# Gated values in three buffers, y's differences one by one, and the third output unit loaded into the first one's place

## The chip, the cores and the metric

The kernel runs on one core of a Trainium2 chip. Its time is the device time in microseconds, the median of several runs. A profile is one more execution, recorded by the hardware profiler; its times hold for that execution.

The engines: TensorE (PE: matrix products, PEld: the weight loads that run beside them), VectorE (DVE), ScalarE (ACT), GpSimd (POOL) and SyncE (SP), whose queue issues nearly all transfers here. Each engine takes its instructions in the order written and waits at the first that is not ready. The order is the program's own (`manual_schedule`), and nothing rearranges it.

## The reference

Three stages on 4608 tokens of 512 values. The inputs are float32.

```
a   = softmax(q k^T / 8) v              # chunks of 64 tokens, 8 heads of 64
x   = reshape(a)                        # 4608 x 512
h   = x @ w_in                          # 4608 x 1024
s   = h * softmax(h)
y   = ((s - mean) / sqrt(var + 1e-6) * g_ln) @ w_out      # 4608 x 512
u   = silu(y @ w_gate) * (y @ w_val)                      # 4608 x 1536
out = u @ w_out2                                          # 4608 x 512
```

Every product is split for precision: each factor is kept as a high part and the rest, and three of the four products of the parts are added up (`PASSES`). The two products of the last stage are in addition formed by Strassen's scheme in Winograd's form: seven block products in place of eight, from sums and differences of blocks.

## The kernel before, in words

Up to about 315 us the kernel forms attention, h and the normalized s; to 523 us it multiplies by w_out (`y_run`, in runs of 24 products of 128x128 by 128x384) and meanwhile prepares the weights of the last stage. The change concerns what comes then.

**The gated stage, 72 steps (`step`, L925).** The tokens lie in six groups s of 768 and the 1536 columns in twelve blocks f; a step (s, f) makes one block of u for one group. TensorE does seven products of six matmuls each, into the banks psA, psC, psB, psD, psA, psC, psD. The fifth, sixth and seventh add to what the first, second and fourth left in the same bank, so the fifth waits until ScalarE has copied psA to p1 (L934) and the seventh until VectorE has read psD (L941). p1 is one buffer: L934 waits until the step before has read it for the last time (L953). The rest of a step runs beside the products: VectorE adds (L939, L941), GpSimd adds (L942), ScalarE takes the sigmoid of psA into the first half of a tile u (L944), VectorE multiplies (L945), adds psC into the buffer that L942 has read (L948), a second sigmoid (L949), and VectorE ends with L951 to L954. The tile u then goes to memory by one transfer that SyncE issues in the next step (`u_store`, L923). u has two buffers, so L944 waits until the store of two steps ago has read its tile.

**The factors.** The weights of blocks 0, 1 and 2 are loaded once and kept (wc, `cache_load`); the others stream through a ring of three tiles (ws, `w_load`), one load issued whenever a step has used its tile. Group 0 takes blocks 3 to 11 and then 0, 1, 2; the groups after it take 0 to 11. In group 5 all twelve stream, since the space of wc is then used for the factors of the output.

**Beside the steps.** While group s runs, y of group s+1 is loaded (`y_load`) and made into the seven operands of the scheme (`y_units`): for each half kk four differences on GpSimd, called as one unit of four instructions (`sums`, L822), then seven units `split(i, x)`, each with a copy on ScalarE (L825) and a subtraction on VectorE (L826). Sixteen units are spread over the steps, one to three in a step, called after its own instructions:

```
k = -(-len(todo) // ((FT if s < NSG - 2 else 7) - n)) if todo else 0
for x in todo[:k]:
    x()
```

y of group 0 is prepared in the same way during the last eight `y_run`s, two units to a run. The third weight is converted in 24 pieces, one in two steps, from step 0 on: `v_load`, `v_mag` (ScalarE, then L95 on GpSimd), `v_bits` (L101 and L109 on VectorE, then L130 on GpSimd), `v_store`.

**The output stage, 54 units (`unit`).** Unit n = (g, p) reads u of 512 tokens and two blocks from memory (`x_load`), forms four sums on VectorE (`x_sums`, L1042), the high parts on ScalarE (`x_high`, L1048) and the rest on VectorE (`x_low`, L1053), and multiplies (L1119). The x of a unit lies in one of four places: `halves[0]` and `halves[1]` in the tile ry, which y's preparation used before, and two in `hold`, a part of the tile work, which takes the space of the last group's y operands and is free only when the last step's products are done. Unit n takes place n mod 4. Units 0 and 1 are prepared during the last four steps, units 2 and 3 after them. `x_low(n)` ends by calling `x_load(n + 4)`. The loop at the end prepares ahead of the products:

```
for n in range(NU):
    x_high(n + 2)
    x_sums(n + 3)
    x_low(n + 2)
    for i in range(2):
        unit(n, i)
```

Of the kernel before, what the change touches and what calls it, by code (L numbers as in the profile page):

```python
# [8 lines left out]
F32 = mybir.dt.float32  # L9
# [14 lines left out]
def attn_moe_moe2_kernel(  # L24
# [136 lines left out]
    def y_run(wB, i0, i1, ps, sb, ptags=("y",), stag="ysb", queue=nc.scalar):  # L161

        for i in range(i0, i1):
            u, n = divmod(i, NY)
            m, d = divmod(u, KD)
            f, (a, b) = n // 3, PASSES[n % 3]
            if n == 0:
                ys[u] = ps.tile([P, TOK], F32, tag=ptags[u % len(ptags)], name="y")
            nc.tensor.matmul(  # L169
                ys[u], lhsT=wB[:, f, a, d * P:(d + 1) * P], rhs=lnT[m][:, b, f, :],  # L170
                start=(n == 0), stop=(n == NY - 1),
            )
            if n == NY - 1:
                ysb = sb.tile([P, TOK], F32, tag=stag, name="ysb", bufs=3 if stag == "osb" else 2)
                nc.scalar.activation(out=ysb, in_=ys.pop(u), func=AF.Copy)  # L175
                queue.dma_start(out=y_dram[m][d], in_=ysb)
# [588 lines left out]
    with ExitStack() as ph2:  # L765
# [6 lines left out]
        )  # L772
        ry = cpa.tile([P, 3, 4, TOK], F32, tag="ry", name="ry")
        rawy, tt = ry[:, 0:2], ry[:, 2]
        yk = {0: cpa.tile([P, NS, 2, 2, TOK], F32R, tag="yka", name="yka")}
# [35 lines left out]
        def y_units(s, kks=(0, 1)):  # L811

            if s not in yk:
                yk[s] = yk_tile(s)
            dst, units = yk[s], []
            for kk in kks:
                b11, b12, b21, b22 = (rawy[:, kk, i] for i in range(4))
                t1, t2, t3, t4 = (tt[:, i] for i in range(4))

                def sums(b11=b11, b12=b12, b21=b21, b22=b22):  # L820
                    for o, p, q in ((t1, b12, b11), (t2, b22, t1), (t3, b22, b12), (t4, b21, t2)):
                        nc.gpsimd.tensor_tensor(out=o, in0=p, in1=q, op=ALU.subtract)  # L822

                def split(i, x, kk=kk):
                    nc.scalar.activation(out=dst[:, i, 0, kk], in_=x, func=AF.Copy)  # L825
                    nc.vector.tensor_tensor(  # L826
                        out=dst[:, i, 1, kk], in0=x, in1=dst[:, i, 0, kk].bitcast(F32),
                        op=ALU.subtract,
                    )

                units.append(sums)
                for i, x in enumerate((b11, t1, t2, t3, b21, b22, t4)):
                    units.append(lambda i=i, x=x, split=split: split(i, x))
            return units
# [31 lines left out]
        for m in range(1, NG):  # L866
            for d in range(KD):
# [10 lines left out]
                if last_m and d == 0:  # L878
                    stage_.close()
                    p2.close()  # L880
                    cp = ph2.enter_context(pool("cp"))
                    for i in range(3):
                        osb = cp.tile([P, TOK], F32, tag="osb", name="osb", bufs=3)
                    yk[1] = yk_tile(1)
                if last_m and d < RING:
                    w_load()
                for x in ahead_y[:2]:
                    x()
                ahead_y = ahead_y[2:]
                u = (m * KD + d) * NY  # L890
# [29 lines left out]
        def u_store():  # L920
            while pend:
                s, f, u = pend.pop()
                nc.sync.dma_start(out=u_dram[s][f // 2][:, f % 2], in_=u)  # L923

        def step(s, f):  # L925
# [4 lines left out]
            p1, p5, u3 = t384("p1"), t384("p5"), t384("u3")  # L930
            u = cb.tile([P, 2, TOK], F32, tag="u", name="u", bufs=2)
            sa, sb = u[:, 0], u[:, 1]
# [25 lines left out]

        flat = ry.rearrange("p a b n -> p (a b n)")
        halves = [  # L960
# [64 lines left out]
        def x_load(n):  # L1025
            if n >= NU:
                return
            j = n % 4
            x = halves[j] if j < 2 else hold[0][:, (j - 2) * 8:(j - 1) * 8]
            xs[n] = x  # L1030
# [19 lines left out]
        def x_low(n):  # L1050
# [5 lines left out]
            )  # L1056
            x_load(n + 4)

        todo = []
        for s in range(NSG):  # L1060
            for n, f in enumerate([*range(RING, FT), *range(RING)] if s == 0 else range(FT)):
                late = n + FT * (s - NSG + 2)
                G = n + FT * s
                if s == 0 and n in (2, 4, 6):
                    cache_load(n // 2 - 1)
                if s + 1 < NSG:
# [16 lines left out]
                if G % 2 == 0 and 0 <= G // 2 - 1 < 2 * FT:  # L1083
                    v_mag(G // 2 - 1)
                if G % 2 == 0 and G // 2 < 2 * FT:
                    v_load(G // 2)
# [4 lines left out]
                if 8 <= late < 8 + 2 * NFP and late % 2:  # L1091
                    t_split(late // 2 - 4)
                if late in (20, 21):
                    x_sums(late - 20)
                if late in (21, 22):
                    x_high(late - 21)
                    x_low(late - 21)
        u_store()

        work = cp.tile([P, 36, HT], F32, tag="ykb", name="work")  # L1100
        hold[0] = work[:, 0:16]
        sb1s = [work[:, 16 + 2 * i:18 + 2 * i] for i in range(2)]
        oss = [work[:, 20 + 4 * i:24 + 4 * i] for i in range(4)]
        x_load(2)
        x_load(3)
        x_sums(2)
# [84 lines left out]
```

## Time and profile before

| | |
|---|---|
| median of 3 runs | 1351.31 us (1351.18 to 1354.51) |
| the profiled execution | 1348.65 us, of which the span from first to last instruction is 1346.6 us |
| mean granted TensorE clock | 0.997 of full |
| busy, share of the span | PE 97%, PEld 92%, DVE 73%, ACT 46%, POOL 33% |
| transfers | 318.39 MB, mean 236 GB/s |

A busy share is a mean over stages. The gated stage takes 539.3 us of the span (522.8 to 1062.1), the output stage the 284.5 us after it. The idle time of TensorE is listed by the waits of its weight loads, which come ahead of the products that they serve: each line gives the line that waited, the instruction that released it, the sum, the number and the longest. A wait of another engine matters only where it reaches TensorE.

### The profile page before, as it was taken

To read this page: it belongs to the slowest core of one execution; us is meant where nothing else is said; L and a number is where in the kernel's file an instruction comes from. 1 tells how busy PE (TensorE), PEld (TensorE's weight loads), DVE (VectorE), ACT (ScalarE), POOL (GpSimd) and SP (SyncE) were. 2 spreads that over 40 slices of the span, in tenths; PEclk is the share of its full clock that TensorE was granted. 3 is DMA by queue.
4 is the path that set the end of the run, shared out by engine and by line. 5 is a ranking of instruction groups with operands and counts; after the bars stand their busy time and mean duration, and the time that the engine had idled before them with its cause. 6 is when DMAs were issued, how large, how long until landed. Compare 5 with 4: busy or idle time off the path is not lost.

```text
span 1346.6 us, 26266 instructions
## 1 busy us (share of the span) xinstructions
PE 1303.4 (97%) x10054; PEld 1243.4 (92%) x10054; DVE 982.0 (73%) x1672; ACT 617.9 (46%) x1024; POOL 442.6 (33%) x602
## 2 busy tenths in 40 slices
PE   4999999999999999999999999999999999999997
PEld 3788888888999999999999999999999999999997
DVE  7688888885577774576776767667677788877774
ACT  5466666666566563333433333334333333333331
POOL 5355555554243441333323323332432000000111
PEclk9999999999999999999999999999999999999999
DMA  5466555675799997993795995967999444444441
GB/s 211 128 182 188 178 175 174 185 217 172 268 384 351 376 347 297 420 373 130 275 321 208 320 343 194 330 245 248 343 349 341 155 143 140 136 140 142 126 145 59
DMA packets 146541, 318.39 MB, mean 236 GB/s; under 512 B 11248, under 2 KB 94192, under 8 KB 138736
## 3 DMA queue, kind: packets, MB, share of 16 engines
q1 hardware_dynamic: 140080, 308.06, 66.0%
q10 hardware_dynamic: 6336, 8.65, 1.8%
q8 instruction: 79, 1.29, 0.4%
q14 instruction: 46, 0.38, 0.1%
HBM read 225.45 MB, written 91.23 MB: 235 GB/s over the span
## 4 chain that ended last, share of the span: by engine, by line
PE 84%; DMA 4%; DVE 4%; issue 4%; POOL 3%; ACT 1%; SPq 0%; POOLq 0%; ACTq 0%; DVEq 0%
PE y L169 15%; PE h L381 14%; PE pa L909 8%; PE pc L909 8%; PE pd L909 8%; PE opc L1119 6%; PE opb L1119 6%; PE opa L1119 6%; PE pb L909 4%; DMA u<-u 3%; PE so_ps L265 3%; PE opd L1119 3%; PE tr L462 3%; POOL ry L822 1%; PE pt L335 1%
## 5 line engine op out<-in xcount | busy, mean ns | idle before, releaser
L381 PE MATMUL h<-wA,x 128*128 128x512 f32 x864 | 218.7, 401 | 3.2 <-ACT x L361 2.2
L169 PE MATMUL y<-lnT,wB 128*128 128x384 f32 x1152 | 200.7, 334 | 0.6 <-ACT ysb L175 0.6
L169 PEld LDWEIGHTS y<-lnT,wB 128*128 128x128 f32 x1152 | 199.5, 188 | 0.9 <-ACT ysb L175 0.9
L381 PEld LDWEIGHTS h<-wA,x 128*128 128x128 f32 x864 | 158.2, 190 | 35.6 <-ACT x L361 2.5
L942 POOL TENSOR_TENSOR u<-u,p 128x384 f32<-128x384 f32 x72 | 73.0, 1014 | 229.6 <-DVE u L941 218.3
L944 ACT ACTIVATE u<-pa 128x384 f32<-128x384 f32 x72 | 35.4, 492 | 171.8 <-PE pa L909 129.4
L1129 POOL TENSOR_TENSOR work<-work 128x256 f32<-128x256 f32 x36 | 26.4, 745 | 254.6 <-DVE work L1129 254.6
L949 ACT ACTIVATE u<-p 128x384 f32<-128x384 f32 x72 | 37.9, 527 | 117.7 <-DVE p L948 117.7
L945 DVE TENSOR_TENSOR u<-pa,u 128x384 f32<-128x384 f32 x72 | 40.1, 557 | 64.3 <-ACT u L944 64.1
L1048 ACT ACTIVATE hl<-ry 128x1792 fp32r<-128x1792 f32 x28 | 47.7, 1704 | 77.2 <-PE opd L1119 56.7
L1048 ACT ACTIVATE hl<-work 128x1792 fp32r<-128x1792 f32 x26 | 44.3, 1704 | 80.4 <-PE opd L1119 53.3
L909 PE MATMUL pa<-ykb,ws 128*128 128x384 f32 x360 | 72.5, 335 | 2.3 <-ACT p L934 2.3
L909 PE MATMUL pd<-ykb,ws 128*128 128x384 f32 x360 | 72.2, 334 | 0.3 <-DVE u L941 0.3
L909 PE MATMUL pc<-ykb,ws 128*128 128x384 f32 x360 | 72.0, 334 | 0.0
L724 DVE TENSOR_TENSOR lnT<-lr,lnT 128x1536 fp32r<-128x1536 f32 x24 | 47.5, 1978 | 33.0 <-ACT lnT L723 32.1
L909 PE MATMUL pa<-yka,ws 128*128 128x384 f32 x324 | 65.4, 336 | 4.3 <-ACT p L934 4.3
L1053 DVE TENSOR_TENSOR hl<-ry,hl 128x1792 fp32r<-128x1792 f32 x28 | 56.6, 2022 | 16.4 <-ACT hl L1048 16.3
L909 PE MATMUL pd<-yka,ws 128*128 128x384 f32 x324 | 65.1, 335 | 1.6 <-DVE u L941 1.6
L909 PEld LDWEIGHTS pa<-ykb,ws 128*128 128x128 f32 x360 | 63.0, 188 | 3.6 <-ACT p L934 3.6
L909 PE MATMUL pc<-yka,ws 128*128 128x384 f32 x324 | 64.9, 334 | 0.0
L909 PEld LDWEIGHTS pd<-ykb,ws 128*128 128x128 f32 x360 | 63.2, 188 | 0.7 <-DVE u L941 0.7
L948 DVE TENSOR_TENSOR p<-pc,p 128x384 f32<-128x384 f32 x72 | 40.1, 557 | 32.0 <-POOL u L942 30.7
(147 smaller groups left out, 3161.2 us busy)
## 6 DMA issues: line engine op xcount, KB each, us to landing
ws<-ws SPq DMA_DIRECT2D x57, 1792.0 KB, 9.2
u<-u SPq DMA_DIRECT2D x72, 384.0 KB, 6.7
ln<-lt SPq DMA_DIRECT2D x72, 256.0 KB, 3.0
lr<-ln SPq DMA_DIRECT2D x24, 768.0 KB, 7.4
ry<-u SPq DMA_DIRECT2D x56, 256.0 KB, 3.2
work<-u SPq DMA_DIRECT2D x52, 256.0 KB, 3.2
ws<-shi SPq DMA_DIRECT2D x12, 896.0 KB, 9.6
qt<-in_q SPq DMA_DIRECT2D x36, 256.0 KB, 3.6
```

What stands on the lines that cost most here:

```text
L169: nc.tensor.matmul(ys[u], lhsT=wB[:, f, a, d * P:(d + 1) * P], rhs=lnT[m][:, b, f, :], start=(n == 0), stop=(n == NY - 1),)
L265: nc.tensor.matmul(out[b * CH:(b + 1) * CH, c, n], lhsT=lhsT[r, h], rhs=rhs[r, h], start=True, stop=True, tile_position=(c * CH, b * CH),)
L381: nc.tensor.matmul(h[:, n * DM:(n + 1) * DM], lhsT=x[:, a, k, :], rhs=wA[:, n * KD + k, b, :], start=(j == 0), stop=(j == NH // 2 - 1),)
L462: nc.tensor.transpose(tr[:, f, :], so[:, c0:c0 + P], ident)
L724: nc.vector.tensor_tensor(out=lo, in0=x, in1=hi.bitcast(F32), op=ALU.subtract)
L909: nc.tensor.matmul(ps, lhsT=w[:, a, kk * P:(kk + 1) * P], rhs=y[:, b, kk], start=(first and n == 0), stop=(n == 5), skip_group_check=True,)
L942: nc.gpsimd.tensor_tensor(out=u3, in0=u3, in1=p5, op=ALU.add)
L945: nc.vector.tensor_tensor(out=sa, in0=psA, in1=sa, op=ALU.mult)
L948: nc.vector.tensor_tensor(out=c12, in0=psC, in1=p1, op=ALU.add)
L1048: nc.scalar.activation(out=hl[n][:, 0], in_=xs[n][:, 1:8], func=AF.Copy)
L1053: nc.vector.tensor_tensor(out=hl[n][:, 1], in0=xs.pop(n)[:, 1:8], in1=hl[n][:, 0].bitcast(F32), op=ALU.subtract,)
L1119: nc.tensor.matmul(acc[g, i, t][:, half], lhsT=hl[n][:, a, j, i * P:(i + 1) * P], rhs=tw[p][:, j, b], start=(p == x == half == 0), stop=(p ...
```

## The change

Seven edits, quoted below:

- u gets a third buffer; osb, the buffer of the last four results of `y_run`, has two in place of three.
- ry is shortened from twelve to eleven pieces. The third difference is written over b12 in place of a piece of its own.
- The four differences of a half of y become four units, called in turn with the splits: d1, split of b21, d2, split of b11, d3, split of t1, d4, split of t2, then the splits of t3, b22 and t4. There are 22 units to a group, where there were 16. Ahead of group 0 three are called per run in place of two; in the steps the rule for k gives two to a step in groups 1 to 3 of the loop, three in group 0 and up to four in group 4.
- The kept factors wc are loaded at steps 2, 5 and 8 (before: 2, 4, 6).
- Groups 1 to 3 take the blocks in the order 3, 4, 5, 0, 6, 7, 8, 1, 9, 10, 11, 2.
- The conversion of the third weight begins six steps later.
- Units 2 and 3 of the output are loaded into `halves[0]` and `halves[1]`, behind units 0 and 1, and units 4 and 5 into `hold`. `x_sums(1)` and `x_low(1)` come a step later, the latter behind the last step.

```diff
-                ysb = sb.tile([P, TOK], F32, tag=stag, name="ysb", bufs=3 if stag == "osb" else 2)
+                ysb = sb.tile([P, TOK], F32, tag=stag, name="ysb", bufs=2)
...
-        ry = cpa.tile([P, 3, 4, TOK], F32, tag="ry", name="ry")
-        rawy, tt = ry[:, 0:2], ry[:, 2]
+        ry = cpa.tile([P, 11, TOK], F32, tag="ry", name="ry")
+        rawy, tt = ry[:, 0:8].rearrange("p (a b) n -> p a b n", a=2), ry[:, 8:11]
...
-                t1, t2, t3, t4 = (tt[:, i] for i in range(4))
+                t1, t2, t4 = (tt[:, i] for i in range(3))
+                t3 = b12
...
-                units.append(sums)
-                for i, x in enumerate((b11, t1, t2, t3, b21, b22, t4)):
-                    units.append(lambda i=i, x=x, split=split: split(i, x))
...
+                for i in range(4):
+                    units += [sums[i], parts[i - 1 if i else 4]]
+                units += [parts[3], parts[5], parts[6]]
...
-            u = cb.tile([P, 2, TOK], F32, tag="u", name="u", bufs=2)
+            u = cb.tile([P, 2, TOK], F32, tag="u", name="u", bufs=3)
...
-            x = halves[j] if j < 2 else hold[0][:, (j - 2) * 8:(j - 1) * 8]
+            x = halves[j % 2] if j > 1 or n < 2 else hold[0][:, j * 8:(j + 1) * 8]
...
-            x_load(n + 4)
+            x_load(n + 4 if n > 1 else n + 2)
...
+        orders = (
+            (3, 4, 5, 6, 7, 8, 9, 10, 11, 0, 1, 2),
+            (3, 4, 5, 0, 6, 7, 8, 1, 9, 10, 11, 2),
+            range(FT),
+        )
...
-                G = n + FT * s
-                if s == 0 and n in (2, 4, 6):
-                    cache_load(n // 2 - 1)
+                G = n + FT * s - 6
+                if s == 0 and n in (2, 5, 8):
+                    cache_load(n // 3)
...
-                if late in (20, 21):
-                    x_sums(late - 20)
-                if late in (21, 22):
-                    x_high(late - 21)
-                    x_low(late - 21)
+                if late in (20, 22):
+                    x_sums(late // 2 - 10)
+                if late == 21:
+                    x_high(0)
+                    x_low(0)
+                if late == 22:
+                    x_high(1)
         u_store()
+        x_low(1)
...
-        x_load(2)
-        x_load(3)
+        x_load(4)
+        x_load(5)
```

The first place is GpSimd's queue in group 3, at the first half of y of group 4. L942 (L950 in the changed kernel) is the step's own addition, L95 and L130 belong to the weight's conversion, L822 are y's differences. Before:

```order
L130 TENSOR_TENSOR vm<-vm,vraw 128x256
L822 TENSOR_TENSOR ry<-ry 128x384 x4
L942 TENSOR_TENSOR u_9708<-u_9708,p_9707 128x384
L95 TENSOR_SCALAR vm<-vm 128x256
L942 TENSOR_TENSOR u_9784<-u_9784,p_9783 128x384
```

The same place in the changed kernel:

```order
L130 TENSOR_TENSOR vm<-vm,vraw 128x256
L822 TENSOR_TENSOR ry<-ry 128x384
L950 TENSOR_TENSOR u_9678<-u_9678,p_9677 128x384
L95 TENSOR_SCALAR vm<-vm 128x256
L822 TENSOR_TENSOR ry<-ry 128x384
L950 TENSOR_TENSOR u_9755<-u_9755,p_9754 128x384
```

Four differences stood between two additions; now one stands between any two of them.

The second place is VectorE's queue from the end of the last step into the output stage. L1042 (L1050) are `x_sums`, L1053 (L1061) `x_low`, hl the finished operand of a unit. Before:

```order
L954 TENSOR_TENSOR u_12116<-u3_12115,u_12116 128x384
L1042 TENSOR_TENSOR work_12175<-work_12175 128x256 x8
L1053 TENSOR_TENSOR hl_12184<-work_12175,hl_12184 128x1792
L1042 TENSOR_TENSOR ry_5073<-ry_5073 128x256 x4
L1053 TENSOR_TENSOR hl_12243<-work_12175,hl_12243 128x1792
```

The same place in the changed kernel:

```order
L962 TENSOR_TENSOR u_12112<-u3_12111,u_12112 128x384
L1061 TENSOR_TENSOR hl_12103<-ry_5073,hl_12103 128x1792
L1050 TENSOR_TENSOR ry_5073<-ry_5073 128x256 x8
L1061 TENSOR_TENSOR hl_12183<-ry_5073,hl_12183 128x1792
L1050 TENSOR_TENSOR work_12174<-work_12174 128x256 x4
```

`x_low(1)` (hl_12103) has moved from the step before to here. In both kernels the sums of units 2 and 3 (x8) stand ahead of `x_low(2)` (hl_12184, hl_12183).

The third place is SyncE's queue at the same point, where L1031 and L1032 (L1039 and L1040) are the two transfers of an `x_load`. Before:

```order
L923 DMA u5_5_5066<-u_12116 128x768
L1031 DMA work_12175<-u0_2_5033 128x2x256
L1032 DMA work_12175<-u0_2_5033 128x2x256
L1031 DMA work_12175<-u0_3_5034 128x2x256
L1032 DMA work_12175<-u0_3_5034 128x2x256
```

The same place in the changed kernel:

```order
L1039 DMA ry_5073<-u0_2_5033 128x2x256
L1040 DMA ry_5073<-u0_2_5033 128x2x256
L931 DMA u5_4_5065<-u_11971 128x768
L931 DMA u5_5_5066<-u_12041 128x768
L931 DMA u5_5_5066<-u_12112 128x768
L1039 DMA ry_5073<-u0_3_5034 128x2x256
L1040 DMA ry_5073<-u0_3_5034 128x2x256
```

The load of unit 2 has moved ahead of the last three stores of u; the load of unit 3 stands behind them as before, and waits for `x_low(1)`, which reads what it overwrites.

## Rows read from the trace of the kernel before

**Rows 1.** Waits of the weight loads, whole span: sum us, times, longest us.

```profile
PEld pa L909 <- ACT p L934: 12.2, 9, 3.1
...
PEld pd L909 <- DVE u L941: 3.3, 4, 1.1
PEld opa L1119 <- DVE hl L1053: 2.3, 1, 2.3
```

**Rows 2.** Stretches: length, busy PE PEld DVE ACT POOL, granted clock, DMA share, GB/s.

```profile
522.80:1062.10 539.30, 527.96 (x3025) 523.66 (x3024) 380.41 (x706) 196.28 (x415) 169.90 (x184) 1.00 0.80 289
```

**Rows 3.** Timeline of one undisturbed step: start us, us, what, [idle before <- releaser].

```profile
1039.69 1.20 PE L909 MATMUL pa<-ykb,ws 128*128 128x384 f32 x6
...
1041.29 0.55 DVE L954 TENSOR_TENSOR u<-u,u 128x384 f32<-128x384 f32 x1
1041.47 0.49 ACT L934 ACTIVATE p<-pa 128x384 f32<-128x384 f32 x1 [1.44 <-DVE u L953]
...
1043.85 1.20 PE L909 MATMUL pa<-ykb,ws 128*128 128x384 f32 x6
```

**Rows 4.** ScalarE's waits in the gated stage, 520 to 1065 us.

```profile
ACT u L944 <- DMA u<-u: 35.7, 9, 5.4
```

**Rows 5.** Timeline in group 2, from a late store of u to TensorE's wait.

```profile
718.65 0.49 ACT L944 ACTIVATE u<-pa 128x384 f32<-128x384 f32 x1 [4.43 <-DMA u<-u]
...
723.99 4.06 POOL L822 TENSOR_TENSOR ry<-ry 128x384 f32<-128x384 f32 x4
...
729.05 0.56 DVE L948 TENSOR_TENSOR p<-pc,p 128x384 f32<-128x384 f32 x1 [3.93 <-POOL u L942]
...
732.06 1.16 PE L909 MATMUL pa<-yka,ws 128*128 128x384 f32 x5 [1.82 <-ACT p L934]
```

**Rows 6.** Timeline in group 1, four differences without a late store.

```profile
668.71 0.56 DVE L948 TENSOR_TENSOR p<-pc,p 128x384 f32<-128x384 f32 x1 [2.44 <-POOL u L942]
...
671.73 1.31 PE L909 MATMUL pa<-ykb,ws 128*128 128x384 f32 x6 [0.33 <-ACT p L934]
```

**Rows 7.** Tile u, 520 to 1080 us: duration ns min/median/max, first and last start.

```profile
L941 DVE TENSOR_TENSOR u<-pd,p x72: 557/558/561, 527.1 to 1060.2; 128x384 f32<-128x384 f32 x72
...
L954 DVE TENSOR_TENSOR u<-u,u x72: 543/551/1371, 531.6 to 1064.0; 128x384 f32<-128x384 f32 x72
...
DMA to landing us min/median/max: 2.3/6.0/13.6
```

**Rows 8.** Line L822: duration ns min/median/max.

```profile
L822 POOL TENSOR_TENSOR ry<-ry x48: 987/1015/2268, 490.3 to 920.4; 128x384 f32<-128x384 f32 x48
```

**Rows 9.** Line L176, the stores of y: time to landing.

```profile
DMA to landing us min/median/max: 1.8/6.0/8.7
```

**Rows 10.** Timeline from the last steps into the output stage.

```profile
1053.71 1.31 PE L909 MATMUL pd<-ykb,ws 128*128 128x384 f32 x6 [0.34 <-DVE u L941]
...
1057.59 2.02 DVE L1053 TENSOR_TENSOR hl<-ry,hl 128x1792 fp32r<-128x1792 f32 x1
...
1062.14 0.87 PE L1119 MATMUL opa<-tw,hl 128*128 128x256 f32 x6
...
1065.03 0.61 SPq L1031 DMA_DIRECT2D work<-u  x1
...
1071.45 1.55 DVE L1042 TENSOR_TENSOR work<-work 128x256 f32<-128x256 f32 x4 [0.87 <-DMA work<-u]
...
1074.99 1.22 PE L1119 MATMUL opa<-tw,hl 128*128 128x256 f32 x4 [2.08 <-DVE hl L1053]
```

**Rows 11.** Two stretches with TensorE idle, and behind an idle time.

```profile
903.00:905.00 2.00, 0.00 (x0) 0.00 (x0) 0.00 (x0) 0.54 (x2) 1.92 (x3) 1.00 0.49 181
1075.00:1079.00 4.00, 4.00 (x21) 4.00 (x22) 3.96 (x8) 1.70 (x1) 0.00 (x0) 0.57 0.46 131
```

**Rows 12.** Transfers by form: number, KB each, median us to landing.

```profile
work<-u SPq DMA_DIRECT2D x52, 256.0 KB, 3.2
```

More of the change, by code (lines that the diff above doesn't have):

```diff
@@ L817, in y_units, with diff @@
                 b11, b12, b21, b22 = (rawy[:, kk, i] for i in range(4))
-                t1, t2, t3, t4 = (tt[:, i] for i in range(4))
-                def sums(b11=b11, b12=b12, b21=b21, b22=b22):
-                    for o, p, q in ((t1, b12, b11), (t2, b22, t1), (t3, b22, b12), (t4, b21, t2)):
-                        nc.gpsimd.tensor_tensor(out=o, in0=p, in1=q, op=ALU.subtract)
+                t1, t2, t4 = (tt[:, i] for i in range(3))
+                t3 = b12
+                def diff(o, p, q):
+                    nc.gpsimd.tensor_tensor(out=o, in0=p, in1=q, op=ALU.subtract)
                 def split(i, x, kk=kk):
@@ L829, in split @@
                     )
-                units.append(sums)
-                for i, x in enumerate((b11, t1, t2, t3, b21, b22, t4)):
-                    units.append(lambda i=i, x=x, split=split: split(i, x))
+                parts = [
+                    lambda i=i, x=x, split=split: split(i, x)
+                    for i, x in enumerate((b11, t1, t2, t3, b21, b22, t4))
+                ]
+                sums = [
+                    lambda a=a, diff=diff: diff(*a)
+                    for a in ((t1, b12, b11), (t2, b22, t1), (t3, b22, b12), (t4, b21, t2))
+                ]
+                for i in range(4):
+                    units += [sums[i], parts[i - 1 if i else 4]]
+                units += [parts[3], parts[5], parts[6]]
             return units
@@ L881, in attn_moe_moe2_kernel @@
                     cp = ph2.enter_context(pool("cp"))
-                    for i in range(3):
-                        osb = cp.tile([P, TOK], F32, tag="osb", name="osb", bufs=3)
+                    for i in range(2):
+                        osb = cp.tile([P, TOK], F32, tag="osb", name="osb", bufs=2)
                     yk[1] = yk_tile(1)
@@ L886, in attn_moe_moe2_kernel @@
                     w_load()
-                for x in ahead_y[:2]:
+                for x in ahead_y[:3]:
                     x()
-                ahead_y = ahead_y[2:]
+                ahead_y = ahead_y[3:]
                 u = (m * KD + d) * NY
@@ L957, in step @@
                 w_load()
-        flat = ry.rearrange("p a b n -> p (a b n)")
+        flat = ry.rearrange("p a n -> p (a n)")
         halves = [
@@ L1056, in x_low @@
             )
-            x_load(n + 4)
+            x_load(n + 4 if n > 1 else n + 2)
         todo = []
+        orders = (
[3 more added lines that the diff above has]
+        )
         for s in range(NSG):
-            for n, f in enumerate([*range(RING, FT), *range(RING)] if s == 0 else range(FT)):
+            for n, f in enumerate(orders[min(s, 1) if s < NSG - 2 else 2]):
                 late = n + FT * (s - NSG + 2)
-                G = n + FT * s
-                if s == 0 and n in (2, 4, 6):
-                    cache_load(n // 2 - 1)
+                G = n + FT * s - 6
+                if s == 0 and n in (2, 5, 8):
+                    cache_load(n // 3)
                 if s + 1 < NSG:
@@ L1084, in attn_moe_moe2_kernel @@
                     v_mag(G // 2 - 1)
-                if G % 2 == 0 and G // 2 < 2 * FT:
+                if G % 2 == 0 and 0 <= G // 2 < 2 * FT:
                     v_load(G // 2)
```

## The prediction, made before the changed kernel was run

> **What bounds the kernel now.** I read first who waited for whom, with TensorE's weight loads as the ones that wait, because TensorE is busy nearly everywhere and only its gaps can be given back. Three kinds of gap touch the code of the change [rows 1]. The fifth product of a step waits for the copy of psA (12.2 us, nine times), the seventh for VectorE's reading of psD (3.3 us, four times), and one product of the output stage for its operand (2.3 us). No row of this stage has TensorE wait for a transfer.
>
> A second view checks the first two sums. The gated stage lasts 539.3 us [rows 2]. In an undisturbed step the first and the fifth product begin 4.16 us apart [rows 3], so a product takes 1.04 us, a step of seven 7.28 us, and 72 steps 524.2 us. The stage loses 15.1 us; the waits say 15.5.
>
> The timelines then say why. The copy to p1 is late because the step before it ended late, for two reasons. Nine times the sigmoid L944 had to wait for a store of u, 35.7 us in all [rows 4]. And four differences of y hold GpSimd for 4 us just when the step needs its own addition L942 there. Without a late store such a block makes L948 2.4 us late, and TensorE hardly feels it, 0.33 us [rows 6]. With one, both add up: L948 is 3.9 us late and TensorE stands for 1.8 us [rows 5].
>
> **The gated stage, part by part.** *The third buffer.* A store can be issued when L954 ends, 1041.29 + 0.55 = 1041.84, which is 2.15 us after its next step began [rows 3]. The sigmoid that writes the same tile again is due when the fifth product is done, 1043.85 + 1.20, or 5.4 us into a step [rows 3]. With two buffers this is the step after, which leaves 7.28 + 5.4 - 2.15 = 10.5 us; with three it is 17.8 us. The slowest of these stores landed after 13.6 us [rows 7]. All nine waits of L944 should end.
>
> *The differences one by one.* One takes 1.0 us [rows 8]. The slack of a step is seen in the undisturbed one: the copy to p1 ends at 1041.96 and is needed at 1043.85, 1.9 us later [rows 3]. Four together cost 2.4 us of lateness [rows 6]; one alone is 3 us less, so nothing is late, and a pair (called in two steps of group 0 and three of group 4) should come 2.4 - 2.0 = 0.4 us late, inside the slack. Their sum on GpSimd is unchanged. Behind a difference in GpSimd's queue stand L942 and the weight's conversion; for L942 waits VectorE's L948, whose successors end in the copy to p1. What the slack does not cover is a step with two differences, two splits and the conversion together, which before had no equal. I bound what is left by nothing from below and, from above, by the longest wait that VectorE has caused here, 1.1 us [rows 1], in each of the five steps: 5.5 us. I take 0.5 us, near the row without a late store, which has more differences than any pair.
>
> *The last wait of the seventh product*, in the step from 1053 on [rows 10], comes when `x_sums(1)` and `x_low(0)` follow each other on VectorE. They now lie in different steps, so it goes, and I expect no new one: `x_low` alone takes 2.02 us [rows 10].
>
> Here a page speaks against the change. VectorE's L954 has a median of 0.55 us and a maximum of 1.37, while L941 never exceeds 0.56 [rows 7]; L954 reads two operands from SBUF, L941 one of its two from PSUM. The Trainium skill, SBUF — State Buffer, section SBUF: two separate sides, says that GpSimd and VectorE take a pair of ports in turn for a whole instruction, and that a VectorE instruction with two SBUF inputs is held back entirely. The rows agree: the excess is 0.8 us, nearly a difference. By that rule forty differences now stand beside forty ends of steps, where ten blocks did before. It gives the slower rival below and does not enter the sum, because VectorE is busy for 380 of the 539 us [rows 2].
>
> *Edits that I cost at nothing.* The order with the kept factors between the streamed ones: a load is issued when a tile of the ring falls free and has two whole steps, 14.6 us, in the old order, and three, 21.8 us, in the new one; TensorE waited for none before. If that cover failed, a late load would cost its lateness. The later loads of wc and the later conversion take transfers out of the first steps, where the stores were latest; the conversion now ends in the second half of group 4, well ahead of the last use of its data. Two buffers for the last results of `y_run`: the copies come 4.2 us apart (24 products of 384 columns, four times 1.04), so a store has 8.3 us; it took 6.0 in the median and 8.7 at most [rows 9]. Were it late, ScalarE would stand for 0.4 us, and the first copy to p1 has more than that. t3 over b12 orders nothing anew: b12 has been read by then.
>
> The stage gives back 15.5 - 0.5 = 15.0 us.
>
> **The output stage.** Unit 2 costs two things now: 2.3 us of waiting [rows 1], and behind it four microseconds at a granted clock of 0.57 [rows 11], which lose 4 x 0.43 = 1.7 us. Together 4.0 us.
>
> The change loads unit 2 early, but VectorE's order keeps the wait alive. `x_low(2)`, which finishes unit 2, stands behind `x_sums(3)`; that needs the load of unit 3; that load overwrites unit 1 and must wait for `x_low(1)`; and `x_low(1)` now stands behind the last step. In numbers: the output stage starts at 1062.14 [rows 10]; the last L954 ends 2.15 us later, at 1064.3, as in the undisturbed step; `x_low(1)` takes 2.02, to 1066.3. It is wanted in unit 1, which begins 5 us after unit 0 (four half units lie between 1062.14 and the wait of unit 2 at 1072.7, the 2.3 us before 1074.99), so this one is in time by about 1 us. The load of unit 3 takes from 0.6 for its first issue [rows 10] plus 3.2 for the second's landing [rows 12], 3.8 us, to the 5.1 us that the same load took before: the fourth and third issue followed two of 0.6 us after 1065.03, and `x_sums(3)` began at 1071.45 [rows 10]. So `x_sums(3)` begins at 1070.1 to 1071.4, takes 1.55, and `x_low(2)` ends at 1073.7 to 1075.0. Against 1072.7 the wait is 1.0 to 2.3 us. I take 1.6, since fewer loads stand in front of this one, and no fall of the clock; a fall costs up to 1.7 more. The output stage gives back 4.0 - 1.6 = 2.4 us, with bounds of nothing and 3.0.
>
> On the clock the rows leave it open. An idle time of 2.7 us around 904 left the granted clock at 1.00; that of 2.1 us at 1073 was followed by 0.57 over four microseconds [rows 11], at the lower level of 1.2 GHz for most of them. [...]
>
> **Sum.** 15.0 + 2.4 = 17.4 us. The profiled execution took 1348.65 us, of which 2.05 lie outside the span of 1346.6; it would come to 1331.2. The median of the runs is 1351.31, 2.7 us above the profiled one, and I carry the same offset over: 1333.9 us.
>
> **Rivals.** *Half of it stays.* Steps with pairs, splits and conversion become the new limit (5.5 us left) and unit 2 gains nothing because the load of unit 3 takes the long price: 15.5 - 5.5 = 10.0 us, 1341.3 us. For it: rows 6 show a slack nearly used up. Against: every pair is shorter than the block there.
>
> *The stores are not what makes L944 wait.* If a transfer in front of them in SyncE's queue is what is late, the third buffer only moves the wait, and the differences alone act. Without late stores a block costs 0.6 us or less as it is, so at most 5 us are won, 1346 us, about no change. For it: stores wait in one queue with loads. Against: five late ones lie where wc is loaded, and 17.8 us exceed the worst landing.
>
> *Slower.* The ends of steps lose to GpSimd's port. Each of the forty differences holds back L952 to L954 of its step by up to 0.8 us [rows 7], and the split behind them again. If this passed the slack of 1.9 us in every step with a difference, TensorE would lose the excess forty times; from 17.4 / 40 = 0.43 us each it eats the gain, and at 0.6 us the kernel takes 1351.3 - 17.4 + 24 = 1358 us. For it: L954's maximum. Against: two delays of 0.8 us stay below 1.9 us, and VectorE catches up in the steps without a difference.
>
> **How the numbers follow.** The forecast, with a clock that falls or not, from 1331 to 1338: 0.72. Half stays: 0.15. About no change: 0.08. Slower: 0.05. A change under 0.3%, 4 us, can't be told from none in this kernel. So faster 0.87, same 0.08, slower 0.05. The range goes from 1330.5 us (both sums whole: 1351.3 - 15.5 - 4.0 = 1331.8, and 1.3 us for the offset of the runs) to 1344 us, which takes in most of the second case.
>
> **What would show it.** After the change the waits of the weight loads in L909's place should come to under 2 us, ScalarE's list should have no wait for a store of u, and L948 (then L956) should wait for GpSimd by less than 1 us anywhere. One wait of 1 to 2.3 us should remain at unit 2, released by VectorE's `x_low`, with `x_sums(3)` in front of it waiting for a transfer. The forecast is wrong if TensorE waits for a load of ws, if the fifth product still waits in groups 1 to 4, or if unit 1 waits for `x_low(1)`.

## The result, and the profile after

| | before | after |
|---|---|---|
| median | 1351.24 us (1349.96 to 1354.51, 4 runs) | 1334.28 us (1334.18 to 1334.92, 4 runs) |
| the profiled execution | 1348.65 us | 1334.26 us |
| its span | 1346.6 us | 1332.4 us |
| gated stage | 539.3 us [rows 2] | 527.9 us |

The ratio is 0.9872, with a 95% interval of 0.9854 to 0.989. The medians are 17.0 us apart, the two profiled executions 14.4 us; the difference between these two numbers is taken up below.

Line numbers move by 8 to 16: L909 is now L917 (the products), L934 L942 (the copy to p1), L941 to L944 L949 to L952, L948 L956, L954 L962, L1042, L1048 and L1053 L1050, L1056 and L1061, L1119 L1135.

First the waits of TensorE's weight loads after the change, 520 to 1100 us (line that waited, releaser: sum us, times, longest us), beside [rows 1]:

```profile
PEld pd L917 <- DVE u L949: 2.2, 3, 1.2
PEld pa L917 <- ACT p L942: 1.8, 1, 1.8
PEld opa L1135 <- DVE hl L1061: 1.4, 1, 1.4
```

The fifth product waits once, where it waited nine times. The gated stage has 2.2 + 1.8 = 4.0 us of waits left of 15.5, so 11.5 are gone, and its length says the same, 539.3 - 527.9 = 11.4 (the window's columns are those of [rows 2]):

```profile
522.80:1050.70 527.90, 525.13 (x3025) 523.85 (x3024) 389.58 (x705) 198.01 (x416) 175.62 (x184) 1.00 0.83 295
```

The two causes that were named are gone. ScalarE's sigmoid, L944 before, now has only this entry in ScalarE's waits of the stage. In the place of [rows 4] stands nothing, although the slowest store landed even later than in [rows 7], after 14.3 us:

```profile
ACT u L952 <- PE pa L917: 173.4, 72, 2.5
```

The tile u, 520 to 1080 us, in the view of [rows 7]:

```profile
L962 DVE TENSOR_TENSOR u<-u,u x72: 544/551/1370, 531.5 to 1052.3; 128x384 f32<-128x384 f32 x72
...
DMA to landing us min/median/max: 2.3/6.1/14.3
```

And VectorE's L956, which [rows 5] showed 3.9 us late behind a block of four differences, waits for GpSimd 1.1 us at most (VectorE's waits, 520 to 1060 us):

```profile
DVE p L956 <- POOL u L950: 9.5, 19, 1.1
```

The 4.0 us that are left have two places. The first, 2.2 us, is three steps of group 4. This is the worst of them, at 909 us (timeline; start us, us, what, idle before and releaser):

```profile
904.27 0.29 DVE L101 TENSOR_SCALAR vm<-vm 128x256 int32<-128x256 int32 x1
...
904.59 0.43 DVE L109 SCALAR_TENSOR_TENSOR vm<-vraw,vm 128x256 int32<-128x256 int32 x1
...
904.93 2.86 DVE L826 TENSOR_TENSOR ykb<-ry,ykb 128x384 fp32r<-128x384 f32 x3
905.09 0.99 POOL L130 TENSOR_TENSOR vm<-vm,vraw 128x256 int32<-128x256 int32 x1 [3.42 <-DVE vm L109]
...
906.05 1.33 POOL L822 TENSOR_TENSOR ry<-ry 128x384 f32<-128x384 f32 x1
...
908.36 0.56 DVE L949 TENSOR_TENSOR u<-pd,p 128x384 f32<-128x384 f32 x1
...
908.97 1.31 PE L917 MATMUL pd<-yka,ws 128*128 128x384 f32 x6 [0.85 <-DVE u L949]
```

VectorE has two instructions of the conversion and three splits to do one after another before the next step's first additions. L949, which must read psD before the seventh product, ends at 908.92, and the product starts at 908.97. There is one difference in this step, not a pair. The three splits take 2.86 us, 0.95 us each, where the median split takes 0.55, and GpSimd works on L130 and a difference beside them.

The other two of the three steps, at 900 and 916 us, wait 0.5 us each. They have two differences, two splits and the half of the conversion that gives VectorE nothing to do (ScalarE and L95 on GpSimd). L95 comes before the two differences, and beside these VectorE's instructions are long again. This is the one at 900 us:

```profile
895.89 2.60 POOL L822 TENSOR_TENSOR ry<-ry 128x384 f32<-128x384 f32 x2
...
896.26 1.37 DVE L962 TENSOR_TENSOR u<-u,u 128x384 f32<-128x384 f32 x1
...
897.55 1.83 DVE L826 TENSOR_TENSOR ykb<-ry,ykb 128x384 fp32r<-128x384 f32 x2
```

The second place, 1.8 us, is the last step:

```profile
1043.72 1.55 DVE L1050 TENSOR_TENSOR ry<-ry 128x256 f32<-128x256 f32 x4
...
1045.36 1.70 ACT L1056 ACTIVATE hl<-ry 128x1792 fp32r<-128x1792 f32 x1 [3.36 <-DVE ry L1050]
1046.96 0.47 ACT L942 ACTIVATE p<-pa 128x384 f32<-128x384 f32 x1
...
1047.48 1.32 PE L917 MATMUL pa<-ykb,ws 128*128 128x384 f32 x6 [1.51 <-ACT p L942]
```

`x_high(1)` (L1056) is called one step before the last. It needs `x_sums(1)`, which VectorE reaches at 1043.72, behind the end of the step before. So ScalarE stands at L1056 for 3.36 us, and the copy to p1 that TensorE needs is queued behind it.

In the output stage, which starts at 1050.73, one wait remains at unit 2, of 1.15 us in the products and 1.4 in the weight loads:

```profile
1052.81 2.02 DVE L1061 TENSOR_TENSOR hl<-ry,hl 128x1792 fp32r<-128x1792 f32 x1
...
1054.89 0.52 SPq L1039 DMA_DIRECT2D ry<-u  x1
...
1058.80 1.56 DVE L1050 TENSOR_TENSOR ry<-ry 128x256 f32<-128x256 f32 x4 [2.51 <-DMA ry<-u]
...
1060.28 2.02 DVE L1061 TENSOR_TENSOR hl<-ry,hl 128x1792 fp32r<-128x1792 f32 x1
...
1062.35 0.74 PE L1135 MATMUL opa<-tw,hl 128*128 128x256 f32 x4 [1.15 <-DVE hl L1061]
```

Read from top to bottom this is the chain of the prediction: `x_low(1)` ends at 1054.83, the load of unit 3 is issued at 1054.89, `x_sums(3)` waits for it until 1058.80, and `x_low(2)` stands behind it. The clock did not fall behind this wait:

```profile
1062.35:1066.00 3.65, 3.65 (x30) 3.65 (x31) 3.62 (x7) 1.71 (x1) 0.00 (x0) 1.00 0.47 146
```

So unit 2 costs 1.4 us where it cost 4.0, and 11.5 + 2.6 = 14.1 us account for the 14.4 us between the two profiled executions.

### The profile page after: what moved, and what is told of

Same layout as the page of the kernel before. It is cut to its first block, busy times and chain, and to the rows that moved or that the text cites. A ratio compares the mean times of both kernels' runs of the same rounds, so it can differ in the third digit from the quotient of the medians.

```text
span 1332.4 us, 26267 instructions
## 1 busy us (share of the span) xinstructions
PE 1298.9 (97%) x10054; PEld 1241.7 (93%) x10054; DVE 993.7 (75%) x1672; ACT 619.5 (46%) x1024; POOL 448.4 (34%) x602
## 4 chain that ended last, share of the span: by engine, by line
PE 92%; DVE 3%; POOL 1%; issue 1%; DMA 1%; ACT 1%; SPq 0%; POOLq 0%; DVEq 0%; ACTq 0%
PE y L169 15%; PE h L381 14%; PE pd L917 11%; PE pa L917 10%; PE pc L917 10%; PE opc L1135 6%; PE opa L1135 6%; PE opb L1135 6%; PE pb L917 5%; PE so_ps L265 3%; PE opd L1135 3%; PE tr L462 3%; PE pt L335 1%; DMA rin<-in_moe_w_in 0%; DVE ykb L826 0%
## 5 line engine op out<-in xcount | busy, mean ns | idle before, releaser
L950 POOL TENSOR_TENSOR u<-u,p 128x384 f32<-128x384 f32 x72 | 73.1, 1015 | 224.7 <-DVE u L949 224.7
L952 ACT ACTIVATE u<-pa 128x384 f32<-128x384 f32 x72 | 35.5, 492 | 173.4 <-PE pa L917 173.4
L1056 ACT ACTIVATE hl<-ry 128x1792 fp32r<-128x1792 f32 x28 | 47.7, 1704 | 83.3 <-PE opd L1135 46.6
L1056 ACT ACTIVATE hl<-work 128x1792 fp32r<-128x1792 f32 x26 | 44.3, 1705 | 75.4 <-PE opd L1135 51.9
L917 PE MATMUL pa<-ykb,ws 128*128 128x384 f32 x360 | 72.2, 334 | 1.5 <-ACT p L942 1.5
L917 PE MATMUL pc<-ykb,ws 128*128 128x384 f32 x360 | 72.0, 334 | 0.0
L917 PE MATMUL pd<-ykb,ws 128*128 128x384 f32 x360 | 72.0, 334 | 0.0
L1061 DVE TENSOR_TENSOR hl<-ry,hl 128x1792 fp32r<-128x1792 f32 x28 | 56.6, 2021 | 13.7 <-ACT hl L1056 13.7
L917 PE MATMUL pd<-yka,ws 128*128 128x384 f32 x324 | 65.2, 335 | 1.3 <-DVE u L949 1.3
L917 PEld LDWEIGHTS pa<-ykb,ws 128*128 128x128 f32 x360 | 63.2, 188 | 1.8 <-ACT p L942 1.8
L917 PE MATMUL pc<-yka,ws 128*128 128x384 f32 x324 | 64.8, 334 | 0.0
L917 PE MATMUL pa<-yka,ws 128*128 128x384 f32 x324 | 64.8, 334 | 0.0
L1061 DVE TENSOR_TENSOR hl<-work,hl 128x1792 fp32r<-128x1792 f32 x26 | 52.6, 2022 | 15.8 <-ACT hl L1056 15.8
L917 PEld LDWEIGHTS pc<-ykb,ws 128*128 128x128 f32 x360 | 63.3, 188 | 0.0
```

Of the source, the lines that this page charges most:

```text
L917: nc.tensor.matmul(ps, lhsT=w[:, a, kk * P:(kk + 1) * P], rhs=y[:, b, kk], start=(first and n == 0), stop=(n == 5), skip_group_check=True,)
L950: nc.gpsimd.tensor_tensor(out=u3, in0=u3, in1=p5, op=ALU.add)
L1056: nc.scalar.activation(out=hl[n][:, 0], in_=xs[n][:, 1:8], func=AF.Copy)
L1061: nc.vector.tensor_tensor(out=hl[n][:, 1], in0=xs.pop(n)[:, 1:8], in1=hl[n][:, 0].bitcast(F32), op=ALU.subtract,)
```

## The experiments

The question was not whether the change helps but which part brings what, where the 4.0 us left in the stage come from, and why the medians differ by 2.6 us more than the profiles.

**The kernel before, profiled again** (no edit).

> The kernel before once more, for a second profile of it. The two profiled executions differ by 14.4 us, the medians by 17.0; the first profile of before lay 2.6 us under its median. If this offset is a stage that varies from execution to execution in before (the granted clock behind the wait of unit 2 or another idle time), this profile shows it there: more than 1.7 us lost behind unit 2 or a clock below 1.00 somewhere in the gated stage, with the same waits of 15.5 us. Rival: the waits in the gated stage themselves vary, and this profile has them 1 us or more away from 15.5.

It took 1353.73 us (span 1351.8, mean clock 0.993 against 0.997), beside seven other runs of the same kernel from 1347.53 to 1355.62. Its weight loads:

```profile
PEld pa L909 <- ACT p L934: 14.3, 11, 3.0
PEld pd L909 <- DVE u L941: 3.3, 4, 1.1
PEld opa L1119 <- DVE hl L1053: 2.0, 1, 2.0
```

Against [rows 1] the gated stage waits 2.1 us longer. Besides, in the gated and the output stage the clock was lower in three stretches of 10 us (0.83 each, so 1.7 us lost in each), where the first profile has one such stretch, 1070 to 1080 (both have another at 30 to 40 us, long before the change):

```profile
730.00:740.00 10.00, 8.07 (x38) 7.76 (x37) 7.78 (x17) 5.05 (x13) 1.45 (x2) 0.83 0.23 72
732.00:736.00 4.00, 3.31 (x12) 3.31 (x13) 3.04 (x7) 1.51 (x4) 1.00 (x1) 0.66 0.25 98
910.00:920.00 10.00, 10.00 (x51) 10.00 (x50) 6.33 (x14) 3.74 (x8) 3.45 (x4) 0.83 0.11 41
1080.00:1090.00 10.00, 9.81 (x69) 9.81 (x70) 9.74 (x16) 3.40 (x2) 0.00 (x0) 0.83 0.49 150
```

The first profile over the same four microseconds, behind the wait of [rows 5]:

```profile
732.00:736.00 4.00, 3.94 (x22) 3.94 (x23) 3.15 (x7) 1.14 (x4) 1.01 (x1) 1.00 0.25 98
```

2.1 us of waiting and two more falls of 1.7 us make 5.5 us; the two executions differ by 5.1. So a wait of some 2 us in this kernel is in some executions paid once more in clock, at a place where in others it is not. Both answers have a part: the clock and the waits themselves vary.

**The third buffer alone.** The blocks of four and the old orders stay (ry is shortened and osb has two buffers, to make the room).

```diff
-            u = cb.tile([P, 2, TOK], F32, tag="u", name="u", bufs=2)
+            u = cb.tile([P, 2, TOK], F32, tag="u", name="u", bufs=3)
```

> Before with the third buffer of u and with what makes room for it (ry of eleven pieces, t3 over b12, osb of two), differences still in blocks of four, old orders, old loading of the units. Theory (late stores and blocks add up): no wait of L944 for a store; of the 15.5 us the 5.0 of the first steps go, each of the three doubled waits (6.9) falls to that of a block alone, 0.6, the single blocks keep 0.6 each, the last 0.7 stays. Left 5 to 6 us, so 9.5 to 10.5 us faster than before in the profile. Rival (the stores are held by what stands in front of them): L944 still waits, and less than 5 us are won. Unit 2 keeps its 2.3 us and the risk of the clock.

1340.03 us (1338.3 to 1341.02), ratio 0.9898 (0.9881 to 0.9915). No sigmoid waits for a store, and the gated stage keeps 7.4 us:

```profile
PEld pa L910 <- ACT p L935: 5.7, 7, 1.8
...
PEld pd L910 <- DVE u L942: 1.7, 2, 1.1
```

So L944 had been waiting for its tile, and the wait went and did not move, as the rival had it. Why single stores land late this run does not show. What is left is more than the 5 to 6 us expected. Six of the seven waits of the fifth product are 0.6 to 0.7 us long, the price of a block without a late store (in [rows 6] the products show 0.33 of it, the weight loads 0.65), but the seventh, in group 4, is 1.8.

**The single differences alone**, with two buffers of u and the old orders.

```diff
-                units.append(sums)
-                for i, x in enumerate((b11, t1, t2, t3, b21, b22, t4)):
-                    units.append(lambda i=i, x=x, split=split: split(i, x))
+                for i in range(4):
+                    units += [sums[i], parts[i - 1 if i else 4]]
+                units += [parts[3], parts[5], parts[6]]
```

> Before with the differences as single units alone (22 units, three to a run of y ahead of group 0), u in two buffers. Theory: L944 keeps its waits for stores (some 35 us in nine), the first steps keep 5.0 us, the last step 0.7; the single blocks' 2.5 us go and the doubled waits fall from 6.9 to under 1.5, because a late store alone is 2 us of lateness against 1.9 of slack. Left 6 to 7.5 us, so 8 to 9.5 us faster. Rival (only the stores matter): the doubled waits stay above 4 us and less than 5 us are won.

1342.18 us (1341.14 to 1342.73), ratio 0.9914 (0.9898 to 0.9931). Waits of the weight loads:

```profile
PEld pd L916 <- DVE u L948: 3.9, 5, 1.1
PEld pa L916 <- ACT p L941: 2.8, 3, 2.4
```

ScalarE's waits in the same kernel:

```profile
ACT u L951 <- DMA u<-u: 31.0, 8, 5.9
```

31.0 us of late stores, nearly as much as in [rows 4], leave 6.7 us of TensorE's waits, `pd` and `pa` together, and 1.4 are left when the stores are no longer in the way (next run). So late stores cost 5.3 us here. Beside blocks of four they cost 15.5 less the 7.4 that the blocks keep without them, 8.1 us. About a third of their cost needed the block beside them.

**Both together, the rest as before** (old order of blocks, conversion from step 0, units loaded as before).

> Before with both, the third buffer and single differences, but the old orders, the old time of the weight's conversion and the old loading of the units. Theory: the gated stage keeps only the 0.7 us of the last steps and at most 1 us besides, so 13.5 to 15 us faster than before, which is more than the changed kernel won in this stage (11.5 us), since the 1.8 us at the late x_high(1) and the 2.2 us of group 4 are not there. Rival (the orders and the later conversion are needed too): L944 waits again in the first steps or TensorE waits for a transfer, and the gain is under 12 us.

1335.38 us (1332.85 to 1336.07), ratio 0.986 (0.9839 to 0.9882). In the gated stage 1.4 us are left (the waits for `pd` and `pa`):

```profile
PEld opa L1127 <- DVE hl L1061: 2.1, 1, 2.1
PEld pd L917 <- DVE u L949: 0.7, 1, 0.7
PEld pa L917 <- DMA ws<-ws: 0.5, 1, 0.5
PEld pa L917 <- ACT p L942: 0.2, 1, 0.2
```

These two edits take 14.1 of the 15.5 us; one alone took 8.1 and the other 8.8, so by this count 2.8 us of waits needed both causes. Unit 2 still waits 2.1 us here, and the clock falls behind it (0.83 from 1060 to 1070). The gated stage is better than in the changed kernel, which keeps 4.0 us, so some other edit of the change costs time there.

**The change with two buffers of u.**

```diff
-            u = cb.tile([P, 2, TOK], F32, tag="u", name="u", bufs=3)
+            u = cb.tile([P, 2, TOK], F32, tag="u", name="u", bufs=2)
```

> The changed kernel with u in two buffers again, all else of the change kept. Theory (the third buffer ends the waits for stores): L944 (now L952) waits for stores again, at the first steps and at the start of a group, more than 15 us in all; TensorE loses 2 to 6 us more than in the changed kernel's gated stage (4.0 us). Rival (the later loads of wc, the later conversion and the spread order already make the stores land in time): under 8 us of such waits, and TensorE loses less than 1 us more.

1338.36 us (1336.21 to 1339.5), ratio 0.9896 (0.9879 to 0.9912). The profile waits 2.2 us more than that of the change (`pa` 4.0 for 1.8):

```profile
PEld pa L917 <- ACT p L942: 4.0, 4, 1.8
PEld pd L917 <- DVE u L949: 2.2, 3, 1.1
```

ScalarE's waits for the stores:

```profile
ACT u L952 <- DMA u<-u: 26.0, 8, 6.2
```

The profiled executions are 1.95 us apart (1336.21 and 1334.26), the medians 4.1. In waits of TensorE the third buffer is worth 2.2 us here, 5.3 beside single differences with the rest as before, and 8.1 beside blocks of four. Which of the other edits takes it from 5.3 to 2.2 no run separates.

**The change with the old order of blocks** and the kept factors loaded at steps 2, 4 and 6.

```diff
-            for n, f in enumerate(orders[min(s, 1) if s < NSG - 2 else 2]):
+            for n, f in enumerate(orders[0 if s == 0 else 2]):
...
-                if s == 0 and n in (2, 5, 8):
-                    cache_load(n // 3)
+                if s == 0 and n in (2, 4, 6):
+                    cache_load(n // 2 - 1)
```

> The changed kernel with the old order of the blocks (kept factors first in groups 1 to 3) and wc loaded at steps 2, 4 and 6. Theory (the order costs and brings nothing, since a streamed factor has time enough either way): waits of the gated stage within 0.7 us of the changed kernel's 4.0, time within 2 us of it. Rival (the spread is what lets the stores and loads land): L952 waits for stores in spite of three buffers, or TensorE waits for a load of ws by more than 1 us.

1334.38 us (1334.25 to 1335.75), ratio 0.9866 (0.9851 to 0.988), and the three waits of the change to the tenth. With three buffers and the later conversion, the order and the later loads of wc neither bring nor cost anything.

**The change with the conversion from step 0.**

```diff
-                G = n + FT * s - 6
+                G = n + FT * s
```

> The changed kernel with the conversion of the third weight begun at step 0 as in before, all else kept. Theory (the 2.2 us of group 4 come from the conversion meeting two differences and two splits in one step): the waits of the seventh product in group 4 fall from 2.2 us to under 0.5; in the first steps, with more transfers at once, at most 0.7 us appear; 1.5 to 2.2 us less waiting in all. Rival (four units in a step are too many by themselves): the waits in group 4 stay above 1.5 us.

1332.19 us (1331.8 to 1334.16), ratio 0.985 (0.9835 to 0.9865). The 2.2 us of group 4 are gone:

```profile
PEld pa L917 <- ACT p L942: 1.8, 1, 1.8
PEld opa L1135 <- DVE hl L1061: 1.2, 1, 1.2
```

The differences and splits of group 4 are the same as in the change, pairs included. So it was the conversion, moved six steps later into the group where the splits are densest. The timeline shows in what way. These are L962 and the two splits of the step at 900 us, then the three splits of the worst step, which took 1.37, 1.83 and 2.86 us in the change:

```profile
896.74 0.55 DVE L962 TENSOR_TENSOR u<-u,u 128x384 f32<-128x384 f32 x1
...
897.20 1.01 DVE L826 TENSOR_TENSOR ykb<-ry,ykb 128x384 fp32r<-128x384 f32 x2
...
903.37 1.49 DVE L826 TENSOR_TENSOR ykb<-ry,ykb 128x384 fp32r<-128x384 f32 x3
```

With the conversion in these steps, VectorE's same instructions took longer beside GpSimd's. In the worst step VectorE's own L101 and L109 (0.7 us) go as well; what each is worth there no run separates.

**The change with `x_high(1)` behind the last step.**

```diff
-                if late == 22:
-                    x_high(1)
+        x_high(1)
         u_store()
         x_low(1)
```

> The changed kernel with x_high(1) called behind the last step in place of ahead of it. Theory (the 1.8 us wait in the last step is ScalarE standing at x_high(1) for x_sums(1), with the copy to p1 behind it): that wait goes, unit 1 stays in time (its x_low was behind the last step anyway), the wait at unit 2 stays at 1.0 to 1.8 us: 1.5 to 2 us faster than the changed kernel in the profile. Rival (VectorE's x_sums(1) itself is in the way): 1 us or more remains in the last step, or unit 1 waits for its operand.

1332.85 us (1332.21 to 1333.51), ratio 0.9852 (0.9837 to 0.9867). The wait of the last step is gone, the other two stay:

```profile
PEld pd L917 <- DVE u L949: 2.2, 3, 1.1
PEld opa L1134 <- DVE hl L1061: 1.4, 1, 1.4
```

**The change again**, as the neighbour of the two that follow.

> The changed kernel once more, beside the next two on the same chip, to have its times and a second profile for the comparison. Waits as in its first profile: 4.0 us in the gated stage, 1.0 to 1.8 us at unit 2. If its runs scatter much less than those of before (which go from 1347.5 to 1355.6 us), the theory that the scatter comes from falls of the clock behind the long waits gains: none of its waits reaches 2 us.

1334.96 us (1334.06 to 1335.95), ratio 0.9881 (0.9866 to 0.9895); waits of 2.2, 1.8 and 1.3 us.

**The change with `x_low(2)` ahead of `x_sums(3)`.**

```diff
             x_high(n + 2)
-            x_sums(n + 3)
-            x_low(n + 2)
+            if n == 0:
+                x_low(n + 2)
+                x_sums(n + 3)
+            else:
+                x_sums(n + 3)
+                x_low(n + 2)
```

> The changed kernel with x_low(2) ahead of x_sums(3) in the first round of the output loop, nothing else. Theory (x_low(2) is ready and stands behind x_sums(3), which waits for the load of unit 3): the wait of 1.4 us at unit 2 goes, none comes at unit 3, and the profile is 1.2 to 1.5 us shorter. Rival (the high part of unit 2, or the loading, is late by itself): 0.5 us or more remains at unit 2 or turns up at unit 3.

1332.6 us (1332.47 to 1332.7), ratio 0.9863 (0.9849 to 0.9877). The wait at unit 2 is gone and no other came for it:

```profile
PEld pd L917 <- DVE u L949: 2.2, 3, 1.2
PEld pa L917 <- ACT p L942: 1.8, 1, 1.8
```

**All three mendings together**: the conversion from step 0, `x_high(1)` behind the last step, `x_low(2)` first.

> All three mendings together: x_high(1) behind the last step, x_low(2) ahead of x_sums(3), the conversion of the third weight from step 0. If the three waits (1.8, 1.4 and 2.2 us) are independent, the gated stage and the first units of the output have no wait of TensorE above 0.3 us left, and the time is 5.0 to 5.6 us below the changed kernel's, about 1329 us. Rival (time won at one place is lost at the next): waits of 1 us or more remain, and the gain is under 4 us.

1330.01 us (1328.64 to 1330.69, 5 runs), ratio 0.984 (0.9825 to 0.9854): 4.95 us under the change run beside it, a trace below the 5.0 to 5.6 expected, and the fastest kernel here. Its profiled execution, the slowest of the five, is 3.6 us under that of the change beside it; its gated stage begins 1.5 us later (at 524.2 for 522.7 us), which no edit explains. Between 520 and 1100 us one wait is left, where none above 0.3 us was expected; the run with both edits alone had one of the same length:

```profile
PEld pa L917 <- DMA ws<-ws: 0.5, 1, 0.5
```

and of 570 us TensorE is busy for 569.81:

```profile
520.00:1090.00 570.00, 569.81 (x3392) 569.40 (x3391) 424.73 (x761) 215.18 (x429) 178.64 (x188) 1.00 0.81 288
```

## Why the prediction was right, and where it was not

*The third buffer, and the sum of a late store and a block.* Right. All nine waits of L944 ended, with stores that land as late as before. Each half removes about half of the waits (8.1 and 8.8 of 15.5 us), both 14.1. The rival, by which the third buffer only moves the wait, is refuted by the third buffer alone: the waits ended and 8.1 us went. What makes single stores land late stays open.

*"I take 0.5 us."* This step failed. The gated stage kept 4.0 us, 3.5 more than that, and this is what the sum missed: 17.4 us forecast between the profiled executions, 14.4 measured. It has two parts.

The first is the later conversion. I put it among the edits that cost nothing, because it "ends in the second half of group 4, well ahead of the last use of its data". That looked at the deadline alone. What it does in group 4, where there are up to four units to a step, I had seen ("two differences, two splits and the conversion together") and bounded at 5.5 us, but then I took the value of a row that holds no conversion. Two of the three steps are the meeting that I had named (0.5 us each). The worst is another, three splits with a single difference; its 1.2 us even pass the 1.1 that I had set as the most for one step. In all three VectorE's instructions were longer than in the median, which no term of the sum has. 2.2 us measured, and 0 with the old start of the conversion.

The second is "I expect no new one" in the last steps. I followed `x_sums` and `x_low` on VectorE, and they do lie apart now. I did not follow `x_high(1)`, which kept its step while the `x_sums(1)` that it needs moved to the same one. On ScalarE it stands ahead of the copy to p1, and the products' wait of 0.34 us [rows 10] was exchanged for one of 1.51 (0.7 for 1.8 in the weight loads).

*Unit 2.* Right, mechanism and size. 1.4 us were left where 1.6 were forecast. The load took 3.9 us, from the first issue to the start of `x_sums(3)`, between the bounds of 3.8 and 5.1, and with `x_low(2)` first the wait is gone. The clock did not fall, so the stage gave back 2.6 us (forecast 2.4).

*The order of blocks and the two osb buffers.* Costed at nothing; nothing was seen of them.

*The slower rival.* Wrong as a forecast of the time, but its mechanism is in the 2.2 us. L962 has the same maximum as L954 in [rows 7], 1370 for 1371 ns. In most steps the slack takes this up. In the three steps of group 4 VectorE's instructions were 1.2 to 1.8 us longer in sum than at the same places without the conversion, and there TensorE waited. So leaving the hold out of the sum, because VectorE is busy for 380 of 539 us, was the use of a mean where single steps decide. The Trainium skill, SBUF — State Buffer, section SBUF: two separate sides, agrees with these rows (0.55 us for L962 in the median, 1.37 beside differences); that the shared ports are what lengthens the instructions is argued from the page, no run shows it.

*The signs.* Two of those named failed with this step: the weight loads in L909's place wait 4.0 us where under 2 were to be left, and L956 waits for GpSimd up to 1.1 us where it was to be less than 1. The other signs came: no sigmoid waits for a store, no weight load for ws, the fifth product waits in the last step alone, unit 1 does not wait.

*The offset of 2.7 us.* It was carried over without a cause, and this hid the error of the sum: 1333.9 forecast, 1334.28 measured, although the profiled execution came out 3.1 us above the 1331.2 worked out. That the median was met within 0.4 us is luck, two errors that cancel. The second profile of before shows a cause: waits that vary, and falls of the clock behind them. The changed kernel has three small places of waiting, no fall of the clock in its profile from the start of the gated stage to 1320 us, runs from 1334.06 to 1335.95 in both series, and no offset (1334.26 and 1334.28). Of 23 other executions of before the granted clock is on record: the six at 0.995 or more took 1350.8 us in the mean, the twelve at 0.993 or less 1353.1. So falls of the clock have a part there too; how much the waits add, and where, is not shown.

## What to carry to other kernels

When work is moved, its data's deadline is only half of the question: for each engine that it passes, list what is queued behind it there, and compare the new sum of that step, not of the mean step, with the step's slack. Take the durations from rows in which the other engine is at work too: a split takes 0.55 us in the median and took 0.95 in the worst step, beside GpSimd. Two delays that each fit into the slack can add up to a wait, and then removing either one gains much of what both gain; the worth of an edit therefore depends on which others are in. Where the runs of a kernel scatter by more than its profile explains, take a second profile before carrying an offset over.

## What was not expected of the hardware

The same kernel, at the same place and with the same work, idled for about 2 us and was granted the full clock afterwards in one execution (1.00 from 732 to 736) and a lower one in another (0.66, which means the lower of its two levels, 1.2 GHz, for most of the four microseconds). In the same way 2.7 us of idling at 904 left the clock at 1.00 in the first profile, where [rows 11] show the idle time and this row what came behind it, while the second has 0.83 from 910 to 920 after a wait at the same place:

```profile
905.00:909.00 4.00, 3.59 (x21) 3.59 (x22) 2.72 (x5) 1.24 (x3) 3.73 (x4) 1.00 0.02 4
```

At unit 2 four of the five profiles with a wait of 1.8 to 2.3 us in the weight loads show a fall behind it (all but that of the third buffer alone), and none of the six with 1.2 to 1.4 us does. So what a wait costs in clock could not be read from one execution; each fall lost 1.7 us here.
